# Issuing V chunks under a queue limit, and a longer lag for the Q/K loads, in a scheduled attention and expert kernel

## The chip, the cores and the metric

The kernel runs on one core of one Trainium2 chip. The metric is the device time of one execution in microseconds (us), the median of several. TensorE is called PE, VectorE DVE, ScalarE ACT, GpSimd POOL and SyncE SP in the profile.

## The reference, cut to what matters

Eight batches, eight heads, 576 positions, head width 64. Attention has a decay from `f`; each batch is then sent through one of eight two-layer experts, chosen by its mean.

```python
q, k, v: (8, 8, 576, 64)   f: (8, 8, 576)   x: (8, 576, 512)   w1: (8, 512, 1024)   w2: (8, 1024, 512)
scores = q @ k.T / 8 ;  cum = cumsum(log(clip(f)))
scores = where(causal, -1e9, scores + cum[i] - cum[j])
attn = softmax(scores) ;  x = attn @ v             # heads side by side: 512 columns
e_idx = argmax(x.mean(positions) @ w_gate)         # one expert for each batch
out = gate * (relu(x @ w1[e_idx]) @ w2[e_idx])
```

## The kernel before

Heads are worked in 16 groups of four (a "quad"; two quads to a batch, four "exps" to a quad). A quad goes through these steps: DVE transposes K and Q; PE makes scores into one shared buffer (`ps_s`, "s=1" below); ACT takes the exp and so frees that buffer; POOL masks it; POOL weighs V by the decay; PE multiplies the masked exps with V ("PV"). Each batch then has a first expert layer (`H`, line L535) and a second (`O`, L550). While one batch's layers run, the next batch's quads run in between.

The order of all of this is decided when the kernel is built. Every operation is an `Op` with an engine, an estimated duration, what it comes after, and a priority. A class `Order` runs a model of the engines and of the DMA queues, and emits instructions in the order in which they start in that model. `behind` means "not before that other operation has been issued".

```python
FILL = 60.0
PM0 = 10.0
LAG = 2
# ... in Order:
    def can(self, op, now):            # are the buffers that op takes free?
        need = {}
        for ring, key in op.takes:
            need[ring] = need.get(ring, 0) + 1
            if ring in self.turn and self.turn[ring][0] != key:
                return False
        return all(sum(t <= now for t, _ in self.free[r]) >= n for r, n in need.items())
# ... a DMA's landing is modelled by self.queues[e]: one list for SP, ACT and POOL each
    RINGS = dict(raw=4, qt=2, vf=2, vb=3, e=2, lr=3, x=4, w=3, h=2, o=6, s=1, bank=4, gate=4)
```

V of a batch is loaded in five chunks of positions: c0, c2 and c4 are issued by SyncE, c1 and c3 by ScalarE. The first four are 256 KB each, in pieces of 256 bytes. Results are stored by SyncE. K, Q and the weights are loaded by GpSimd.

```python
    def load_v(op, b, c):
        eng = nc.scalar if op.engine == "ACT" else nc.sync
        t = VF[od.slot(("vf", b))]
        if c < 4:
            eng.dma_start(t[:, c, :, :], v[b, :, P * c:P * c + P, :].rearrange("h p e -> p h e"))   # L274
        else:
            eng.dma_start(t[64:P, 4, :, :], v[b, :, 512:576, :].rearrange("h p e -> p h e"))        # L276
# ...
            loads_v[b, c] = od.add(f"v{b}{c}", "ACT" if c % 2 else "SP", .4 if c % 2 else .5, lambda op, b=b, c=c: load_v(op, b, c),
                                   prio=6 * b + c * .1 - 8, takes=(("vf", b),) if c == 0 else (), lands=1.4 if c < 4 else .7, grain=.022, ...)
# ... scores (L370), exp (L376), PV (L412), first layer (L535), second layer (L550) are Ops too
            for g in range(5, NQ):     # when quad g's K and Q may be loaded
                raws[g, 1].behind = [ld2] if g < 6 else [wvs[g - LAG][0]]
```

The softmax here doesn't subtract the row's maximum and nothing guards it: scores larger than these inputs give would overflow.

## Time and profile before

| | before |
|---|---|
| time, median (lowest to highest) of 3 | 266.82 us (265.76 to 266.83) |
| span of the profiled run | 263.9 us |
| PE busy | 235.2 us, 89% |
| PE idle after 41 us, all gaps | 15.2 us |
| ACT waiting for a DMA, before an exp | 4.7 + 4.5 us |

The page of the profile gives the busy time of each engine, then busy tenths in 40 slices of 6.6 us. PEclk is the clock that TensorE was granted, in tenths.

```profile
span 263.9 us, 7930 instructions
PE 235.2 (89%) x3325; PEld 152.6 (58%) x3325; DVE 110.9 (42%) x297; ACT 174.9 (66%) x261; POOL 128.2 (49%) x195
...
PE   7778998939999999499899976799999999999991
...
PEclk9975999988999999799999997999999999999998
```

PE is the busiest engine. It has three holes in mid-kernel: the digits 3, 4 and the 7 6 7 at about 53, 106 and 154 to 166 us. After each, the granted clock dips too.

The list of waits says who made whom wait (total us, times, longest us).

```profile
POOL e L383 <- ACT e L376: 76.9, 34, 8.0
...
PE ps_s L370 <- ACT e L376: 15.1, 12, 4.1
...
DVE kt L361 <- DMA rawk<-in_k_dram: 4.7, 3, 1.8
ACT e L376 <- DMA vf<-in_v_dram: 4.7, 1, 4.7
ACT e L376 <- DMA out_dram<-otile: 4.5, 1, 4.5
```

The largest total, 76.9 us of GpSimd, costs nothing by itself: GpSimd is half idle. The two lines at the bottom are one wait each. An exp reads `ps_s` and no V or output, so it can't depend on these DMAs. What waited was the instruction ahead of it in ScalarE's stream, as ScalarE's timeline shows (start, duration, what; in brackets the idle time before it; ACTq is an issue by ScalarE).

```profile
50.56 0.42 ACT L422 ACTIVATE lr<-lr 128x256 f32<-128x256 f32 x1
55.27 0.37 ACTq L274 DMA_DIRECT2D vf<-in_v_dram  x1
55.70 1.66 ACT L376 ACTIVATE e<-ps_s 128x1792 bf16<-128x1792 f32 x1 [4.71 <-DMA vf<-in_v_dram]
...
101.39 1.66 ACT L376 ACTIVATE e<-ps_s 128x1792 bf16<-128x1792 f32 x1 [0.61 <-PE ps_s L370]
107.16 0.37 ACTq L274 DMA_DIRECT2D vf<-in_v_dram  x1
107.58 1.45 ACT L376 ACTIVATE e<-ps_s 128x1536 bf16<-128x1536 f32 x1 [4.53 <-DMA out_dram<-otile]
```

Both times ScalarE stood before the issue of a V chunk. TensorE's timeline in the first block and in the third hole:

```profile
57.41 0.94 PE L370 MATMUL ps_s<-qt,kt 32*128 32x448 bf16 x8 [4.06 <-ACT e L376]
58.28 2.88 PE L535 MATMUL ps_w<-xT,w1e 128*128 128x288 bf16 x12
...
157.94 0.58 PE L370 MATMUL ps_s<-qt,kt 32*128 32x448 bf16 x8 [1.83 <-ACT e L376]
160.34 0.83 PE L370 MATMUL ps_s<-qt,kt 32*128 32x320 bf16 x16 [1.82 <-ACT e L376]
```

In the first block TensorE lost 4.06 us, then ran twelve matmuls in 2.88 us. In the third hole nothing was blocked. Only scores and exps were left in the order, and these take turns on the one buffer.

The chain that ended last names the two transfers behind the blocks (start, us, what):

```profile
34.76 20.42 DMA vf<-in_v_dram
55.27 0.37 ACTq L274
...
92.62 14.48 DMA out_dram<-otile
107.16 0.37 ACTq L274
```

A V load issued by SyncE at 34.76 held up an issue of ScalarE at 55.27, and a store issued by SyncE at 92.62 held up the one at 107.16.

### The profile page before, as it was taken

What the parts mean: (1) busy time and instruction counts of PE and PEld (TensorE: products, weight loads), DVE (VectorE), ACT (ScalarE), POOL (GpSimd) and SP (SyncE); (2) the same over time, 40 slices, a digit from 0 to 9 for tenths busy, and PEclk for the clock granted to TensorE, in tenths of its full rate; (3) what the DMA queues carried; (4) which work ended last, traced back from release to release, by engine and by line L of the source; (5) the groups of instructions that cost most, each with busy time, mean ns of one, the idle gap of its engine ahead of it and who ended that gap; (6) DMA issues with size and microseconds to landing.
All of it is one profiled execution on the core that took longest, in us unless ns stands there. A gap on an engine that the chain in (4) does not pass through costs nothing.

```text
span 263.9 us, 7930 instructions
## 1 busy us (share of the span) xinstructions
PE 235.2 (89%) x3325; PEld 152.6 (58%) x3325; DVE 110.9 (42%) x297; ACT 174.9 (66%) x261; POOL 128.2 (49%) x195
## 2 busy tenths in 40 slices
PE   7778998939999999499899976799999999999991
PEld 2326636716478646377478622768467756876940
DVE  3974553444045855155148600774057623410000
ACT  2398677658486774586586856678487867754930
POOL 4187099304976492207950638608933772140000
PEclk9975999988999999799999997999999999999998
DMA  6988979991999999954999998695997299049832
GB/s 114 225 136 174 189 112 211 212 225 19 180 264 221 225 217 251 232 131 71 219 251 227 201 224 142 111 255 84 201 259 167 37 211 255 6 66 224 211 102 87
DMA packets 57370, 45.84 MB, mean 174 GB/s; under 512 B 39600, under 2 KB 41648, under 8 KB 57328
## 3 DMA queue, kind: packets, MB, share of 16 engines
q0 software_dynamic: 13584, 26.22, 55.6%
q1 hardware_dynamic: 27104, 14.85, 22.5%
q10 hardware_dynamic: 16640, 4.20, 8.1%
q8 instruction: 28, 0.46, 0.7%
q14 instruction: 14, 0.11, 0.2%
HBM read 62.03 MB, written 9.44 MB: 271 GB/s over the span
## 4 chain that ended last, share of the span: by engine, by line
PE 53%; DMA 21%; ACT 8%; DVE 6%; issue 6%; POOL 4%; POOLq 0%; ACTq 0%; SPq 0%; DVEq 0%
PE ps_w L535 18%; PE ps_w L550 14%; PE ps_w L412 9%; DMA vf<-in_v_dram 8%; DMA rawk<-in_k_dram 7%; PE ps_s L370 7%; DMA out_dram<-otile 5%; ACT e L376 5%; PE ps_w L553 2%; PE ps_w L492 2%; ACT e L379 2%; DVE kt L361 2%; DVE qt L361 1%; POOL vb L396 1%; PE ps_w L612 1%
## 5 line engine op out<-in xcount | busy, mean ns | idle before, releaser
L376 ACT ACTIVATE e<-ps_s 128x1792 bf16<-128x1792 f32 (+2 forms) x61 | 91.9, 1507 | 31.1 <-PE ps_s L370 18.0
L383 POOL TENSOR_SCALAR_AFFINE_SELECT e<-e 128x512 bf16<-128x512 bf16 x64 | 41.4, 650 | 80.6 <-ACT e L376 76.9
L535 PE MATMUL ps_w<-xT,w1e 128*128 128x288 bf16 x512 | 74.4, 295 | 1.6 <-DMA w1e<-in_moe_w_dram 1.1
L535 PEld LDWEIGHTS <-w1e 128*128 128x128 bf16 x512 | 61.5, 143 | 11.0 <-issue 5.0
L550 PE MATMUL ps_w<-w2e,h1T 128*128 128x512 bf16 x256 | 60.1, 384 | 0.0
L428 DVE SCALAR_TENSOR_TENSOR xT<-ps_w,lr 128x256 bf16<-128x256 f32 (+1 forms) x64 | 26.9, 454 | 56.7 <-ACT lr L422 55.9
L370 PE MATMUL ps_s<-qt,kt 32*128 32x448 bf16 (+3 forms) x728 | 34.2, 291 | 15.6 <-ACT e L376 15.1
L543 ACT ACTIVATE h1T<-ps_w,gate_b 128x288 bf16<-128x288 f32 x72 | 35.4, 500 | 13.2 <-PE ps_w L535 12.6
L541 DVE TENSOR_SCALAR h1T<-ps_w,gate_b 128x288 bf16<-128x288 f32 x56 | 28.0, 511 | 32.7 <-PE ps_w L535 32.7
L550 PEld LDWEIGHTS <-h1T 128*128 128x128 bf16 x256 | 23.3, 98 | 29.6 <-issue 4.2
L370 PEld LDWEIGHTS <-kt 32*128 32x128 bf16 x768 | 16.5, 96 | 35.5 <-issue 32.9
L412 PE MATMUL ps_w<-e,vb 128*32 128x320 bf16 (+4 forms) x1024 | 29.6, 257 | 2.4 <-DVE xT L428 1.2
L562 ACT COPY otile<-ps_w 128x512 f32<-128x512 f32 (+1 forms) x29 | 15.8, 546 | 23.8 <-PE ps_w L550 22.6
L396 POOL TENSOR_TENSOR vb<-vf,WF 128x512 bf16<-128x512 f32 x29 | 30.5, 1053 | 0.4
L412 PEld LDWEIGHTS <-vb 128*32 128x32 bf16 x1024 | 22.3, 100 | 5.5 <-issue 3.5
L361 DVE STREAM_TRANSPOSE kt<-rawk 128x576 f32<-128x576 f32 x16 | 20.0, 1250 | 7.6 <-DMA rawk<-in_k_dram 4.7
L515 POOL DMA_DIRECT2D w1e<-in_moe_w_dram x14 | 10.4, 743 | 20.4 <-DVE gate_b L506 15.3
L361 DVE STREAM_TRANSPOSE qt<-rawq 128x576 f32<-128x576 f32 x16 | 19.9, 1246 | 0.0
L412 PE MATMUL ps_w<-e,WB 128*32 128x192 bf16 (+4 forms) x512 | 17.8, 261 | 0.4 <-ACT lr L417 0.2
L417 ACT ACTIVATE lr<-ps_w 128x256 f32<-128x256 f32 (+1 forms) x32 | 13.2, 414 | 6.4 <-PE ps_w L412 6.3
L612 PE MATMUL ps_w<-still 128*128 128x512 bf16 x55 | 15.8, 433 | 1.4 <-DVE still L289 1.4
L412 PEld LDWEIGHTS <-WB 128*32 128x32 bf16 x512 | 10.6, 99 | 9.0 <-issue 7.1
(55 smaller groups left out, 144.3 us busy)
## 6 DMA issues: line engine op xcount, KB each, us to landing
out_dram<-otile SPq DMA_DIRECT2D x32, 256.0 KB, 7.4
w1e<-in_moe_w_dram POOLq DMA_DIRECT2D x14, 512.0 KB, 7.5
w2e<-in_moe_w_dram POOLq DMA_DIRECT2D x14, 512.0 KB, 13.5
rawk<-in_k_dram POOLq DMA_DIRECT2D x16, 288.0 KB, 10.7
rawq<-in_q_dram POOLq DMA_DIRECT2D x16, 288.0 KB, 11.8
vf<-in_v_dram ACTq DMA_DIRECT2D x16, 256.0 KB, 9.3
vf<-in_v_dram SPq DMA_DIRECT2D x16, 256.0 KB, 10.2
vf<-in_v_dram SPq DMA_DIRECT2D x8, 128.0 KB, 9.3
```

The source lines that it names most:

```text
L361: nc.vector.transpose(dst, raw)
L370: nc.tensor.matmul(ps[h][:, col:col + i1 - i0], kt[32 * h:32 * h + 32, KLO[c]:KLO[c] + P, r], qt[32 * h:32 * h + 32, i0:i1, r], start=(r = ...
L376: nc.scalar.activation(e, PS_S[:, :, 0:WIDTH[s]], AF.Exp, scale=0.125)
L383: nc.gpsimd.affine_select(out=e[:, :, 0:128], in_=e[:, :, 0:128], pattern=[[0, 4], [1, 128]], channel_multiplier=-1, base=0, compare_op=AL ...
L396: eng.tensor_tensor(vb[:, c, :, :], vf[:, c, h, :], WF[:, b, c, h].unsqueeze(3).to_broadcast([P, 2, 4, D]), op=ALU.mult)
L412: nc.tensor.matmul(ps[32 * h:32 * h + 32, lo - i0:hi - i0], lhs, e[s][:, h, col:col + hi - lo], start=(n == 0), stop=(n == len(parts) - 1) ...
L428: nc.vector.scalar_tensor_tensor(XT[od.slot(("x", b))][:, mm, i0:i1], ps[:, 0:i1 - i0], LN_SCALE, LR[od.slot(("lr", (g, blk)))][:, 0:i1 - ...
L535: nc.tensor.matmul(ps[:, 0:288], lhs, xT[:, m, 288 * half:288 * half + 288], start=(m == 0), stop=(m == 3))
L541: nc.vector.tensor_scalar(dst, ps[:, 0:288], g[:, 0:1], 0.0, op0=ALU.mult, op1=ALU.max)
L543: nc.scalar.activation(dst, ps[:, 0:288], AF.Relu, scale=g[:, 0:1])
L550: nc.tensor.matmul(ps, h[:, j, P * sb:P * sb + P], r, start=(j == 0), stop=(j == 7))
L612: od.filler = lambda i: nc.tensor.matmul(PS_W[i], still[:, 0:P], still[:, 0:512])
```

## The change

The intent as stated: a V chunk goes to a hardware queue only while that queue holds at most two others, so that the issue does not block ScalarE; and the Q/K loads are held back by three quads, not two. (In the code, K and Q of quad g now wait for the weighing of V of quad g - 3 in place of g - 2, so they may be issued one quad earlier.) `runs` is a size that counts against RUNS for each queue of the scheduler's model: 64 for a V chunk (32 for c4), 8 for a store. By these sizes the limit of 130 is tighter than the stated intent: a full chunk is issued while its queue holds at most one other full chunk and no store (64 + 64 = 128). The limit acts on the model's queues when the order is built. No work is added or removed; only the order can change.

```diff
+RUNS = 130
-LAG = 2
+LAG = 3
 ...
     def can(self, op, now):
         need = {}
+        if op.runs and sum(q[3].runs for q in self.queues[op.engines[0]]) + op.runs > RUNS:
+            return False
 ...
-             ... lands=1.4 if c < 4 else .7, grain=.022,                                  # V chunk
+             ... lands=1.4 if c < 4 else .7, grain=.022, runs=64 if c < 4 else 32,
 ...
-             ... lands=.7, grain=.086)                                                    # store
+             ... lands=.7, grain=.086, runs=8)
```

The changed file is three lines longer, so L370, L376, L412, L535 and L550 become L373, L379, L415, L538 and L553.

More of the change, by code (lines that the diff above doesn't have):

```diff
@@ L37, with __init__ @@
 FILL = 60.0
+RUNS = 130
 PM0 = 10.0
-LAG = 2
+LAG = 3
 class Op:
-    def __init__(self, name, engines, us, fn, after=(), prio=0.0, takes=(), gives=(), lands=None, grain=None, behind=()):
+    def __init__(self, name, engines, us, fn, after=(), prio=0.0, takes=(), gives=(), lands=None, grain=None, runs=0, behind=()):
         self.name, self.us, self.fn, self.prio = name, us, fn, prio
@@ L49, in __init__ @@
         self.after, self.takes, self.gives, self.lands = list(after), takes, gives, lands
-        self.end, self.grain = None, grain
+        self.end, self.grain, self.runs = None, grain, runs
         self.other, self.fellow, self.behind, self.issued = (), (), behind, None
@@ L310, in fast_path @@
             loads_v[b, c] = od.add(f"v{b}{c}", "ACT" if c % 2 else "SP", .4 if c % 2 else .5, lambda op, b=b, c=c: load_v(op, b, c), prio=6 * b + c * .1 - 8,
-                                   takes=(("vf", b),) if c == 0 else (), lands=1.4 if c < 4 else .7, grain=.022,
+                                   takes=(("vf", b),) if c == 0 else (), lands=1.4 if c < 4 else .7, grain=.022, runs=64 if c < 4 else 32,
                                    after=[marks[b]] if c == 0 and b in marks else [], behind=[loads_v[b, c - 1]] if c else [])
@@ L610, in fast_path @@
                         takes=(("o", (b, sb)),), gives=(("bank", ("o", b, sb)),))
-            od.add(f"D{b}{sb}", "SP", .5, lambda op, b=b, sb=sb: store(op, b, sb), prio=pm + 3.4 + .5 * n, after=[oc], gives=(("o", (b, sb)),), lands=.7, grain=.086)
+            od.add(f"D{b}{sb}", "SP", .5, lambda op, b=b, sb=sb: store(op, b, sb), prio=pm + 3.4 + .5 * n, after=[oc], gives=(("o", (b, sb)),), lands=.7, grain=.086, runs=8)
     od.filler = lambda i: nc.tensor.matmul(PS_W[i], still[:, 0:P], still[:, 0:512])
```

## The prediction

> **What bounds it now.** From about 131 us on, the chain of waits is almost all TensorE (busy 44.5 of 45 us in the stretch 190:235), so there only TensorE's idle time can be won. By timeline and busy-by-stretch table it stands still three times:
> - 53.3 to 57.4 us: idle 4.06 us; ScalarE did nothing from 51.0 to 55.3.
> - 105.7 to 109.1 us: idle 3.34 us; ScalarE nothing from 103.0 to 107.2.
> - 154 to 166 us: 7.5 of 12 us busy; only score and exp steps were left in the order, alternating on the one score buffer, because the next V product was ordered late.
>
> The waits list gives both ScalarE gaps to a DMA: 4.7 and 4.5 us of idle before an exp. In both, ScalarE's next instruction is a V load. After each pause the granted clock is 0.5 for 3.4 us (12 first-layer matmuls took 2.88 us instead of 1.55). The Trainium skill, "TensorE: Matmul & The Clock Gate", Part 1, says this: half rate after an idle window of about 3.4 us; the trace agrees. So the blocks cost 4.1 + 1.7 and 3.3 + 1.7 us: together nearly 11 us.
>
> **A doubt about the reason.** The blocked issues don't look like a full queue: each carries a semaphore that an earlier transfer still held. The issue at 55.27 uses that of the V load issued at 34.75, which landed at 55.18; the one at 107.16 that of a store issued at 92.61, landed 107.10 (its semaphore wait is 5.7 us long). Eight semaphores rotate over both hardware queues, so an issue waits for the transfer eight before it. SyncE does show issues of 3 to 10 us, perhaps a full queue, but it only delays V and stores.
>
> **What the change moves.** No work is added or removed. In the built order V of batch 3 is issued not all at the 16th exp but at the 20th to 25th, mixed with stores; later V loads also come later and spread out. Their semaphore predecessors are then mostly long landed: neither block should recur. Exposed: ScalarE's loads of batches 4 and 5 near exps 33 to 35, whose predecessors are stores issued only 2 to 3 exps before (0 to 4 us). K/Q loads move one quad earlier (quad 6 at exp 15, not 20, ahead of the second expert's weights), ending delays like the 15.3 us from issue to landing at 68.9 us; TensorE was busy then, so that is worth under 2 us.
>
> Given back: V is used 4 to 5 exps after issue instead of 7 to 16, and hardware V loads take 6 to 25 us under load. The order still has a run of exps with little else (34 to 39, in place of 41 to 48), so I expect the 154 to 166 stall to move, not vanish.
>
> **Sum.** 266.8 - 11 (both blocks) - 1 (K/Q) + 4 (late V, a residual block) = about 259 us; 80% range 251 to 266. Chances: faster by over 2% 0.62, within 2% 0.31, slower 0.07.
>
> **What would show it.** Right: no ScalarE idle over 3 us before an exp with a DMA as releaser before 110 us; two fewer half-clock windows; TensorE busy within 4 us of 235; a score/exp-only stretch near exp 35. Wrong: ScalarE still waiting for a semaphore at a V load, or GpSimd waiting several us for V at its weighing, holding up masks behind it.
>
> **What would make it wrong.** V landing late at batches 3, 4, 5 turns the blocks into V waits (about 265); or the new order fills the 154 to 166 hole too (about 250).

## The result, and the profile after

Ratios are the mean time of one kernel's fast runs over that of the other's fast runs of the same rounds, so they are not quite the ratio of the medians quoted beside them.

| | before | after |
|---|---|---|
| time, median (lowest to highest) of 4 | 266.29 us (264.84 to 266.83) | 255.85 us (255.62 to 257.98) |
| ratio to before | | 0.963 (0.957 to 0.970) |
| span of the profiled run, mean clock | 263.9 us, 0.958 | 253.9 us, 0.964 |
| PE busy | 235.2 us | 230.4 us |
| PE idle after 41 us | 15.2 us | 9.3 us |
| half-clock windows between 50 and 240 us | 3 of 3.4 us | 1 of 6.8 us |

The page of the kernel after:

```profile
span 253.9 us, 7942 instructions
PE 230.4 (91%) x3309; PEld 152.7 (60%) x3324; DVE 108.3 (43%) x293; ACT 176.8 (70%) x265; POOL 128.1 (50%) x195
...
PE   7778988999999999998399899999899999999990
...
PEclk9985899999999999999679999999999999999999
```

The holes at 53 and 106 us are gone, and so is the one at 154 to 166. There is a new one at 120 to 127 us (the digits 8 3, clock 6 7).

Its list of waits:

```profile
POOL e L386 <- ACT e L379: 72.8, 31, 5.9
...
ACT e L379 <- PE ps_s L373: 12.2, 23, 1.0
PE ps_s L373 <- ACT e L379: 9.9, 11, 1.8
DVE kt L364 <- DMA rawk<-in_k_dram: 8.5, 3, 4.7
```

No line of ScalarE waiting for a DMA before an exp is left. On ScalarE's timeline an exp now follows the issue of a V chunk without idle time:

```profile
79.98 0.38 ACTq L277 DMA_DIRECT2D vf<-in_v_dram  x1
80.56 1.66 ACT L379 ACTIVATE e<-ps_s 128x1792 bf16<-128x1792 f32 x1
```

TensorE's longest wait for an exp fell from 4.1 to 1.8 us. DVE's wait for K grew from 4.7 to 8.5 us.

TensorE's timeline in the new hole:

```profile
121.28 0.58 PE L373 MATMUL ps_s<-qt,kt 32*128 32x448 bf16 x8 [1.33 <-ACT e L379]
123.62 0.94 PE L373 MATMUL ps_s<-qt,kt 32*128 32x448 bf16 x8 [1.76 <-ACT e L379]
126.32 0.83 PE L373 MATMUL ps_s<-qt,kt 32*128 32x320 bf16 x16 [1.76 <-ACT e L379]
```

It has the same form as the old hole at 154: scores and exps take turns, until PV products are ready at 127.08. The granted clock is halved from 123.1 on, for 6.8 us. Idle time is 4.85 us.

A third comparison, used for every run below: when does TensorE start the second layer of each batch, read from the first matmuls of that layer in the trace (us)?

| batch | 0 | 1 | 2 | 3 | 4 | 5 | 6 | 7 |
|---|---|---|---|---|---|---|---|---|
| before | 64.2 | 90.5 | 122.4 | 148.2 | 183.1 | 209.3 | 233.9 | 250.0 |
| after | 59.0 | 85.4 | 103.7 | 145.5 | 172.4 | 199.2 | 223.4 | 239.6 |

The gain is 5.2 us at batch 0 and 10.7 at batch 4; from there on nothing more is won or lost. (Batches 2 and 3 stand differently in the two orders, so their columns don't compare.)

The chain after begins differently, as it should when the blocks are gone:

```profile
34.30 6.63 DMA w1e<-in_moe_w_dram
40.97 0.93 PE ps_w L538 x6
41.90 0.51 PE ps_s L373 x7
```

After the first expert's weights it runs through TensorE; the V load and the store are not in it.

### The profile page after: what moved, and what is told of

It reads as the page before. It is cut to its first block, busy times and chain, and to the rows that moved or that the text cites. A ratio compares the mean times of both kernels' runs of the same rounds, so it can differ in the third digit from the quotient of the medians.

```text
span 253.9 us, 7942 instructions
## 1 busy us (share of the span) xinstructions
PE 230.4 (91%) x3309; PEld 152.7 (60%) x3324; DVE 108.3 (43%) x293; ACT 176.8 (70%) x265; POOL 128.1 (50%) x195
## 4 chain that ended last, share of the span: by engine, by line
PE 64%; DMA 14%; ACT 9%; issue 5%; DVE 3%; POOL 2%; POOLq 1%; ACTq 0%
PE ps_w L538 22%; PE ps_w L553 16%; PE ps_w L415 12%; PE ps_s L373 9%; DMA rawk<-in_k_dram 8%; DMA w1e<-in_moe_w_dram 6%; ACT e L379 6%; PE ps_w L556 2%; PE ps_w L495 2%; ACT e L382 2%; DVE h1T L544 1%; PE ps_w L615 1%; ACT otile L565 1%; DVE qt L364 1%; POOLq L514 1%
## 5 line engine op out<-in xcount | busy, mean ns | idle before, releaser
L379 ACT ACTIVATE e<-ps_s 128x1792 bf16<-128x1792 f32 (+2 forms) x61 | 91.9, 1506 | 14.7 <-PE ps_s L373 12.2
L538 PE MATMUL ps_w<-xT,w1e 128*128 128x288 bf16 x512 | 72.6, 290 | 1.4 <-DMA w1e<-in_moe_w_dram 1.0
L538 PEld LDWEIGHTS <-w1e 128*128 128x128 bf16 x512 | 60.5, 142 | 9.5 <-issue 4.7
L553 PE MATMUL ps_w<-w2e,h1T 128*128 128x512 bf16 x244 | 56.2, 379 | 1.5 <-issue 1.3
L373 PE MATMUL ps_s<-qt,kt 32*128 32x448 bf16 (+3 forms) x728 | 34.1, 290 | 10.3 <-ACT e L379 9.9
L544 DVE TENSOR_SCALAR h1T<-ps_w,gate_b 128x288 bf16<-128x288 f32 x58 | 29.3, 513 | 32.9 <-PE ps_w L538 32.2
L565 ACT COPY otile<-ps_w 128x512 f32<-128x512 f32 (+1 forms) x35 | 19.2, 549 | 32.9 <-PE ps_w L553 31.1
L546 ACT ACTIVATE h1T<-ps_w,gate_b 128x288 bf16<-128x288 f32 x70 | 34.5, 500 | 10.5 <-PE ps_w L538 9.8
L553 PEld LDWEIGHTS <-h1T 128*128 128x128 bf16 x256 | 23.7, 98 | 30.1 <-issue 3.5
L373 PEld LDWEIGHTS <-kt 32*128 32x128 bf16 x768 | 16.3, 95 | 28.2 <-issue 25.7
L415 PE MATMUL ps_w<-e,vb 128*32 128x320 bf16 (+4 forms) x1024 | 30.1, 261 | 0.1
L415 PEld LDWEIGHTS <-vb 128*32 128x32 bf16 x1024 | 22.3, 102 | 4.0 <-issue 1.6
L415 PE MATMUL ps_w<-e,WB 128*32 128x192 bf16 (+4 forms) x512 | 18.4, 268 | 0.2
L615 PE MATMUL ps_w<-still 128*128 128x512 bf16 x51 | 15.1, 446 | 2.1 <-DVE still L292 1.4
L415 PEld LDWEIGHTS <-WB 128*32 128x32 bf16 x512 | 10.9, 101 | 8.8 <-issue 6.6
```

The lines of the kernel that those rows point to most:

```text
L373: nc.tensor.matmul(ps[h][:, col:col + i1 - i0], kt[32 * h:32 * h + 32, KLO[c]:KLO[c] + P, r], qt[32 * h:32 * h + 32, i0:i1, r], start=(r = ...
L379: nc.scalar.activation(e, PS_S[:, :, 0:WIDTH[s]], AF.Exp, scale=0.125)
L415: nc.tensor.matmul(ps[32 * h:32 * h + 32, lo - i0:hi - i0], lhs, e[s][:, h, col:col + hi - lo], start=(n == 0), stop=(n == len(parts) - 1) ...
L538: nc.tensor.matmul(ps[:, 0:288], lhs, xT[:, m, 288 * half:288 * half + 288], start=(m == 0), stop=(m == 3))
L544: nc.vector.tensor_scalar(dst, ps[:, 0:288], g[:, 0:1], 0.0, op0=ALU.mult, op1=ALU.max)
L546: nc.scalar.activation(dst, ps[:, 0:288], AF.Relu, scale=g[:, 0:1])
```

## The experiments

Two questions were open. What held ScalarE: a full queue, as the change's intent says, or the completion semaphores? And where do the 10 us come from: the two blocks alone, or the new order too?

**What the trace says on the first.** Each hardware DMA (one issued by SyncE or ScalarE) carries a completion semaphore. In these programs eight of them are used in turn by both engines together. So an issue needs the semaphore of the hardware DMA eight before it in the program. "Slack" here is the time from the landing of that earlier DMA to the issue. No issue of ScalarE in the kernel before has a smaller slack than the three smallest shown; all the others have 5 us or more:

| kernel | issue by ScalarE | DMA eight before | landed | slack |
|---|---|---|---|---|
| before | 49.45 | V load of SyncE, 34.33 | 42.87 | 6.57 |
| before | **55.27** | V load of SyncE, 34.76 | 55.18 | **0.10** |
| before | 81.00 | store, 67.80 | 74.96 | 6.04 |
| before | **107.16** | store, 92.62 | 107.10 | **0.07** |
| before | 135.25 | store, 125.93 | 134.26 | 0.99 |
| after | all after 50 us | | | 2.43 or more |

The wait instruction before the second blocked issue is recorded as well: it names that semaphore (and one more, whose last DMA had landed by 99.39) and lasts 5.73 us, from 101.40. A queue reading does not explain this, since ScalarE's own issues never take over 0.69 us once they start in these two kernels. On SyncE some V issues do take 3 to 10.7 us by themselves, in most cases while two or more V chunks issued there before are still moving (at 75.71 and 105.57 in the kernel before, 3.60 and 3.85 us, it was one, with stores; 70.63 took 10.68 us in the kernel after, in spite of the limit). That does look like a full queue, but it is SyncE's.

All runs below gave correct results. Single kernels scatter by about 1 to 2% from run to run, so differences under 1% are not read.

### The limit alone (LAG stays 2)

```diff
-LAG = 3
+LAG = 2
```

> The changed kernel with K/Q held back by 2 quads again: only the limit on V chunks is left. Its order issues V of batch 3 at the 19th to 20th exp instead of the 16th, so the V loads that held its semaphores have landed. If the blocks at ScalarE are the cost (my theory): no ScalarE idle over 3 us before an exp with a DMA as releaser, and most of the 10.4 us gain: 256 to 261 us; its order has a longer run of exps with no V product (32 to 40), so 1 to 4 us may be given back against the changed kernel. If the K/Q part does the work (rival): 264 us or more.

Measured: 259.77 us (255.88 to 261.60; two of four runs slow), ratio 0.985 (0.973 to 0.996). In the profiled run, at 255.88 us, no issue blocked ScalarE, and the score and exp hole stood at 147 to 154 us with 1.34 + 1.76 + 1.76 us of idle. Second layers started at 171.0 (batch 4) and 240.4 (batch 7), within 1.5 us of the kernel after. So the limit alone takes both blocks away. The timed runs were too scattered to say whether it gives all of the gain.

### The lag alone (no limit)

```diff
-LAG = 2
+LAG = 3
```

> The kernel before with K/Q held back by 3 quads and no limit on V chunks. If the V limit is what pays: ScalarE still waits several us for a semaphore at one or two V loads and the time is 261 to 267 us. If the K/Q part pays by itself, or if any reshuffling of the order moves the blocked loads away: 255 to 260 us. The trace decides between the last two: a ScalarE wait for a DMA gone in spite of bursts of V would mean that the limit is not needed for it.

Measured: 265.35 us (263.76 to 267.56), ratio 1.004 (0.990 to 1.018). The time fell into the first range of the expectation, but for another reason than the one given there: in its trace ScalarE is no longer blocked. Moving the K/Q loads had moved the V issues as well; the ones at 56.06 and 108.40 us had slack of 11 and 13 us, and the one at 58.59 barely escaped, with 0.10. What was won was lost elsewhere. TensorE's timeline of this kernel, in the middle and near the end:

```profile
128.41 0.52 PE L370 MATMUL ps_s<-qt,kt 32*128 32x320 bf16 x16 [1.76 <-ACT e L376]
130.49 0.47 PE L370 MATMUL ps_s<-qt,kt 32*128 32x192 bf16 x16 [1.56 <-ACT e L376]
132.83 2.56 PE L535 MATMUL ps_w<-xT,w1e 128*128 128x288 bf16 x10 [1.87 <-ACT otile L562]
...
240.01 2.38 PE L535 MATMUL ps_w<-xT,w1e 128*128 128x288 bf16 x9 [2.61 <-DMA w1e<-in_moe_w_dram]
```

Its second layers started 4.7 us ahead of before at batch 6 (229.2 against 233.9), but only 0.5 ahead at batch 7 (249.5 against 250.0): the last batch waited 2.61 us for its first-layer weights and then ran 3.4 us at half clock. Between, it had a hole of its own (1.76 + 1.56 + 1.87 us). Over the whole trace TensorE stood idle for 14.9 us after 41 us, against 15.2 before, and between 50 and 245 us the clock was at half for 13.7 us, against 10.2. So "the blocks are gone" is not enough for a gain; the rest of the order has to hold.

### The blocks alone: before's order, every V chunk issued by SyncE

```diff
-        eng = nc.scalar if op.engine == "ACT" else nc.sync
+        eng = nc.sync
```

> The kernel before, every engine's order as it was, but all V loads are issued by SyncE in the same place of its order; ScalarE issues none. If ScalarE standing at its V loads is the cost: TensorE's two pauses at 53 to 57 and 106 to 109 us vanish and the time falls by 7 to 11 us, to 256 to 260 us, with the hole near 154 us still there; V may land later, as one queue carries it all. If the new order of work is what pays and not the blocks: within 3 us of before.

Measured: 258.34 us (257.68 to 260.11), ratio 0.978 (0.966 to 0.990). This is the cleanest measure of the blocks, for the order on every other engine is that of before. Second layers start, against before: 4.7 us earlier at batch 0, 9.4 at batch 2, 9.4 at batch 3, 7.7 at batch 4 and 7.6 at batch 7. So the first block cost 4.7 us and the second another 4.7, and 1.7 us was given back in the old hole, which is still there:

```profile
148.58 0.57 PE L370 MATMUL ps_s<-qt,kt 32*128 32x448 bf16 x8 [1.83 <-ACT e L376]
150.98 0.83 PE L370 MATMUL ps_s<-qt,kt 32*128 32x320 bf16 x16 [1.82 <-ACT e L376]
```

The same two gaps as before's at 157.94 and 160.34, now with half-clock windows of 6.8 and 3.4 us in place of one of 3.4. (The last section says what can make the difference.)

### A block put back by bytes that fill no queue

Into the kernel after: six loads of 32 bytes on SyncE, behind V of batch 3. They move the rotation, but hardly load a queue.

```diff
+    pads = [const.tile([1, 8], fp32, name=f"pad{i}") for i in range(6)]
 ...
+        if b == 3 and c == 4:
+            for t in pads:
+                nc.sync.dma_start(t, f[0, 0:1, 0:8])
```

> The changed kernel with six extra loads of 32 bytes on SyncE behind V of batch 3; they add next to nothing to the queues but turn the eight semaphores on by six, so that ScalarE's second V load of batch 3 (issued at 80.0 us) must wait for a V load on SyncE that landed at 87.4 us. If the rotation of semaphores blocks (my theory): ScalarE stands 5 to 8 us there, TensorE pauses, and the time rises by 2 to 7 us, to 258 to 263 us. If a full queue is what blocks (rival): no wait of ScalarE there and within 1 us of the changed kernel.

Measured: 262.61 us (261.75 to 264.00), ratio 0.995 (0.983 to 1.006) to before, where the kernel after has 0.963 to 0.972. ScalarE's and TensorE's timelines of this kernel (its lines are numbered seven higher than before's; the V load is four higher):

```profile
79.82 0.99 ACT L550 ACTIVATE h1T<-ps_w,gate_b 128x288 bf16<-128x288 f32 x2 [0.40 <-PE ps_w L542]
86.34 0.37 ACTq L278 DMA_DIRECT2D vf<-in_v_dram  x1
86.82 1.66 ACT L383 ACTIVATE e<-ps_s 128x1792 bf16<-128x1792 f32 x1 [6.00 <-DMA vf<-in_v_dram]
```
```profile
88.53 0.83 PE L377 MATMUL ps_s<-qt,kt 32*128 32x320 bf16 x16 [5.30 <-ACT e L383]
```

A block of 6.00 us was made, and TensorE lost 5.30. The six small issues make a staircase that follows the landings of the DMAs eight before, to within 0.03 us once SyncE is past its long V issue:

| issue | at | DMA eight before | landed |
|---|---|---|---|
| SyncE, small load 3 | 83.18 | store, 63.26 | 83.17 |
| SyncE, small load 4 | 84.02 | store, 65.65 | 84.00 |
| SyncE, small load 5 | 84.66 | store, 66.92 | 84.64 |
| SyncE, small load 6 | 85.29 | store, 68.66 | 85.28 |
| ScalarE, V chunk | 86.34 | V load of SyncE, 69.68 | 86.32 |

ScalarE's own queue was empty all this time: its last V issue, at 59.28, had landed by 62.18. This settles it for this block: the semaphore's turn held the issue, not the queue that it goes to.

### Before's first block, moved by the count of small loads

Into the kernel before: five or six 32-byte loads on SyncE, ahead of V of batch 3. With five, the blocked issue should again meet a V load; with six, one of the small loads.

```diff
+    pads = [const.tile([1, 8], fp32, name=f"pad{i}") for i in range(5)]    # or 6
 ...
+        if b == 3 and c == 0:
+            for t in pads:
+                nc.sync.dma_start(t, f[0, 0:1, 0:8])
```

> The kernel before with five extra loads of 32 bytes on SyncE ahead of V of batch 3. The rotation then gives ScalarE's first V load of batch 3 the semaphore of its own V load c3 of batch 2, which landed at 56.5 us, and its second one that of an extra load. If the rotation blocks (my theory): the first block stays and is 1 to 3 us longer, from about 49 to 56.5 us; time 264 to 270 us. If a full queue blocks (rival): the block is as before, 51.0 to 55.3 us, and so is the time.

> The same with six extra loads instead of five: one load of 32 bytes more. Now both of ScalarE's V loads of batch 3 follow extra loads in the rotation. If the rotation blocks (my theory): the first block is gone, TensorE does not pause at 53 to 57 us, and the time falls by 3 to 6 us against before, to 259 to 263 us, the second block (near 100 us) staying. SyncE's own V loads of batch 3 then wait to about 56 us, which should not matter. If a full queue blocks (rival): same as before and as with five.

Measured with five: 266.90 us (264.97 to 270.62), ratio 1.010 (0.995 to 1.024). ScalarE's recorded wait names the predicted semaphores, the last to come being that of its own V load, which landed at 56.74, and takes 6.68 us from 50.08; TensorE's gap is 5.38 us in place of 4.06. As expected; but as that load is ScalarE's own, this run alone would not exclude a full queue of ScalarE. With six, the issue went out at 55.47 while that load was still moving (it landed at 56.74).

Measured with six: 263.79 us (262.92 to 269.68), ratio 0.998 (0.985 to 1.011). The block did not go, against the expectation. ScalarE's timeline with six (lines numbered four higher than before's):

```profile
49.67 0.50 ACT L547 ACTIVATE h1T<-ps_w,gate_b 128x288 bf16<-128x288 f32 x1 [0.29 <-PE ps_w L539]
55.47 0.38 ACTq L278 DMA_DIRECT2D vf<-in_v_dram  x1
55.89 0.38 ACT L421 ACTIVATE lr<-ps_w 128x256 f32<-128x256 f32 x1 [5.72 <-DMA pad<-in_f_dram]
```

The profile names the small load as what held ScalarE. It was issued at 40.30; the issue instruction ended at 41.91; part of its semaphore's count came at 42.12, but the 32 bytes moved at 54.41 and the count was complete at 55.39, and ScalarE's wait for that semaphore ended at 55.41. Four small loads issued by SyncE between 38.94 and 43.01 all moved their bytes at 54.41 to 54.44, so they had stood behind something in SyncE's queue: most likely the V chunks issued just before them, which landed at 43 to 57 us. So a 32-byte transfer can hold an issue for 5 us. The Trainium skill says as much of both halves: "DMA: Bandwidth & Descriptors", section "Queues, rings and completion order", that each DMA engine takes descriptors in ring order; section "Why a DMA increments its semaphore by 16 and not by 1", that the issuer writes at once the counts for the DMA engines that a small transfer doesn't use. The trace agrees, with 42.12 and 55.39 us. The miss was in the expectation's guess of when it lands, not in the rotation.

### The changed kernel again, and with every V chunk on SyncE

```diff
 # after_again: no edit.   after_v_sync:
-        eng = nc.scalar if op.engine == "ACT" else nc.sync
+        eng = nc.sync
```

> The changed kernel itself, on the same chip as the next three, as their yardstick: 255 to 258 us, 3 to 4% under before, with TensorE's one hole near 120 us and no ScalarE wait for a DMA.

> The changed kernel with all V loads issued by SyncE in the same order. As ScalarE no longer waits at V loads in the changed kernel, nothing is left to win: within 2 us of it, unless V on one queue lands later and is missed (then 1 to 4 us slower). A gain of over 2 us would mean that ScalarE's V issues still cost something that I overlooked.

Measured: 257.50 us (256.51 to 261.44, the highest slow), ratio 0.972 (0.960 to 0.985), and 256.43 us (254.25 to 257.87), ratio 0.972 (0.961 to 0.982). No difference: in the new order ScalarE has nothing left to be freed of. This is also what the Trainium skill leads one to expect ("DMA: Bandwidth & Descriptors", section "Issuing engines are not separate DMA queues"): which engine issues changes only sequencer time, and transfers share the same 16 DMA engines. In the order of the kernel before, the same edit was worth 2.2%, because there ScalarE stood waiting for semaphores.

### A looser limit, to fill the hole

In the built order of the kernel after, six to seven exps go by between the PV products of one quad and those of the next, in the worst places; with RUNS=194 and LAG=2 it is at most five after the first batch. So that order should have no hole. It was tried with V on SyncE, with a limit of 170 as well, and with V issued as in the kernel after.

```diff
-RUNS = 130
-LAG = 3
+RUNS = 194        # r170_l2_sync: 170
+LAG = 2
 ...               # r194_l2_sync and r170_l2_sync also:
-        eng = nc.scalar if op.engine == "ACT" else nc.sync
+        eng = nc.sync
```

> Two separate causes, taken on together: V issued by SyncE (no block at ScalarE can come from it), and the limit loosened from 130 to 194 with K/Q held back by 2 quads, an order whose runs of exps without a V product are at most 4 long after the first batch (the changed kernel has one of 7 and one of 6, before one of 7 or more). If the hole near 120 us (4.9 us idle and 6.8 us at half clock) is made by such a run of exps: no hole after 60 us longer than 1 us in sum, and 248 to 253 us. If holes come from somewhere else (late V): 254 to 260 us.

> The same with the limit at 170, another order with runs of at most 5. If the length of the run is what counts: 248 to 254 us, as the one with 194; if the orders differ by chance in what they meet: 250 to 260 us.

> The order of the first of these three, with ScalarE issuing its share of V. In its rotation ScalarE's V loads of batch 5 follow stores issued shortly before them. If the rotation catches it: a ScalarE idle of 2 to 5 us at one of its V loads and 2 to 5 us more than with SyncE; if not: within 1.5 us of it.

Measured: 255.74 us (253.99 to 256.93), ratio 0.961 (0.954 to 0.967); 255.22 us (254.06 to 258.19), ratio 0.959 (0.953 to 0.965); 254.00 us (252.80 to 256.41), ratio 0.954 (0.948 to 0.960). The granted clock of the third, over the slices of the page:

```profile
PEclk9985899999999999999999999999999999999998
```

The hole is gone (from 41 us on, the clock is full up to the last slice), but little came of it. The profiled run of the third starts batch 7's second layer at 240.4, against 239.6 for the kernel after: it is behind by 4.5 us at batch 1 (89.9 against 85.4), where the V chunks go out sooner and smaller gaps stand (1.53 us at 81.4, 1.11 at 88.4), and then wins that back. Two cautions: this trace is of the slowest of the third's six runs (256.41 us; the others took 252.80 to 255.26), and the trace of the first, at 253.99 us, starts batch 7's second layer at 238.4. So filling the hole seems to have cost part of its worth elsewhere; how much is not shown. The first two missed their expected ranges (248 to 253 and 248 to 254 us). The third was not caught by the rotation, as the second branch of its expectation has it. The profiled run with the limit of 170 was slow and is not read.

### The changed kernel, five rounds

> The changed kernel once more, in five rounds, so that its ratio to before has an interval as narrow as those of the three orders of the last call (0.954 to 0.961): 0.963 to 0.972. Below 0.958, those orders are no faster than the change; above 0.965, the one with ScalarE issuing (0.954) is faster by about 1%.

Measured: 256.19 us (255.29 to 258.25), ratio 0.972 (0.965 to 0.978). The hole is at 120.3 to 126.7 us, with the same three gaps as before (1.34 + 1.76 + 1.76). Against this the version with RUNS=194 and LAG=2 has a lower ratio (0.954), and the intervals don't overlap; but the two were timed in different calls, whose runs of the kernel before differ by almost 2 us (267.47 and 265.61), and its one trace, of its slowest run, shows no earlier finish. The medians differ by 2.2 us. It is probably the fastest version here, by 1 to 2%, but this was not tested within the same rounds.

## Why the prediction was right

**That the blocks come from the semaphores' turn, and not from a full queue: right.** Shown by the staircase, where six 32-byte loads put a block back, and by the one block that a 32-byte load held. The stated intent of the change names the wrong cause for ScalarE; the change works because issuing V later and spread among stores leaves each issue of ScalarE with a landed predecessor (slack of 2.43 us or more in the profile, 1.80 in that of after_again). That is a by-product: the limit does not see semaphores, and the lag alone escaped a block by 0.10 us.

**That neither block recurs: right.** ScalarE's two waits of 4.7 and 4.5 us are gone from the list.

**"The blocks cost ... together nearly 11 us": right in kind, a little high.** Measured alone, with before's order, they cost 9.4 us up to batch 3. The estimate was idle time plus half of each 3.4 us window at half clock. Of the half clock the Trainium skill says that it follows one idle window of about 3.4 us ("TensorE: Matmul & The Clock Gate", Part 1), and the trace agrees for the first block, where the 3.4 us just before the half clock were all idle. For the second less was enough: TensorE was busy for 16% of them. How the 1.4 us between 10.8 and 9.4 arise was not measured.

**"K/Q (1)": not seen.** The K load's median time to landing went from 10.7 to 11.0 us, DVE's wait for K grew from 4.7 to 8.5 us, and the chain after still holds a K load of 15.21 us, at 150.94. TensorE's gaps at that time are under 1 us, so this cost little.

**"+ 4 (late V, a residual block)": this is the term of the sum that was mis-sized; it came out near zero.** No residual block came: the predicted candidates near exps 33 to 35 had slack of 8 us and more. GpSimd did not stand for late V, for with only one or two V chunks under way at a time, those issued between 92.8 and 118.0 us landed in 3 to 8 us. By the table of second layers, the kernel after is 3.0 us ahead of the one with the blocks alone taken out (10.7 against 7.7 at batch 4). So 9.4 us were won by the blocks, and about 1.3 us net in these two traces at the hole: the gaps are as large (4.85 + 0.97 us, against 5.6 us in before's order without the blocks), but the old hole drew 10.2 us of half clock there, and the new one 6.8. That these 1.3 us belong to the new order is not shown. With the same gaps the old hole drew only 3.4 us in the kernel before, and the new one 3.4 us in after_again; and the timed ratios overlap (0.978, 0.966 to 0.990, for the blocks alone; 0.972, 0.965 to 0.978, for the kernel after in five rounds). So the removal of the blocks is what is shown to pay.

**"I expect the 154 to 166 stall to move, not vanish ... near exp 35": right.** It moved to 120 to 127 us. The busy times by stretch show the old one and the new (us from and to, length, then busy us and count of each engine, and the granted clock). Of the kernel before, and of the kernel after:

```profile
154.00:166.00 12.00, 7.46 (x80) 2.98 (x79) 0.29 (x1) 7.31 (x8) 7.70 (x12) 0.86 0.87 165
```
```profile
119.00:127.00 8.00, 3.14 (x51) 1.36 (x49) 2.99 (x4) 5.10 (x6) 7.66 (x11) 0.76 1.08 212
154.00:166.00 12.00, 12.00 (x279) 9.08 (x279) 5.24 (x18) 10.35 (x17) 7.15 (x11) 1.00 1.12 250
```

TensorE (the first busy figure) was idle 4.5 of 12 us in the old hole, and 4.9 of 8 in the new one; the old place is full.

**"TensorE busy within 4 us of 235": right, though the profile says 230.4.** That trace lacks 12 of 256 matmuls of L553. The two other profiled runs of the same kernel, after_again and after_five, have all 3,324 matmuls and show 231.5 and 232.0 us, within 4. Most of what is left comes from the clock: between 50 and 240 us TensorE was busy at half clock for 9.3 us before, and for 2.9 and 3.8 us in those two, which by half of the difference (an estimate) is about 3 us.

**"two fewer half-clock windows": right by count, 3 and then 1, but the one is twice as long.** In time it is 10.2 and then 6.8 us (3.4 in after_again).

What stays open: how much of the gain the lag adds to the limit. Alone it gave nothing, and the limit alone scattered by 2%.

## What to carry to other kernels

When an engine stands at a DMA issue, look up which semaphore the wait names and which earlier transfer holds it: it may belong to another queue, and a 32-byte load can hold it as well as a large one. Then issue from an engine off the critical path, or put the issue where the transfer that many places before has long landed. And after a wait is removed, look where TensorE idles next: of the orders without the blocks, one gained nothing, because, by its trace, a hole elsewhere and a late weight load took it back.

## What the Trainium skill lacked or had wrong

- "DMA: Bandwidth & Descriptors", section "Issuing engines are not separate DMA queues", says that the sequencer's time to initiate a DMA is usually small relative to the DMA itself. The issue instruction on ScalarE took 0.37 us here, but the wait for a completion semaphore still held by an earlier DMA (in four of the five blocks looked at here, one of SyncE) took 4.5 to 6.7 us of a compute engine. Neither this page nor any other that was consulted tells of completion semaphores being taken in turn by both issuing engines (eight of them in this program), nor that an issue then waits for the DMA eight before.
- The same page gives no depth at which an issue itself becomes slow. On SyncE, V issues of 128 or 256 KB in 256-byte pieces took 3 to 10.7 us (70.63 us in the kernel after: 10.68), mostly when two or more V chunks issued there were still moving. The cause of these was not tested.
- "TensorE: Matmul & The Clock Gate", in its closing table, advises no idle gaps over about 3 us, and its Part 1 speaks of one idle window. Here the clock was halved for 6.8 us from 123.1 us on with no gap over 1.76 us: TensorE was busy for 3.14 of 8 us in that stretch. The page's section on PSUM-queue cycling does say that frequent short idle times make the clock oscillate, but gives no share. The 13 traces of fast runs give one, counted from 42 us to 16 us before the end: the clock changes on a fixed grid of 3.41 us. Of the windows at full clock, all 17 in which TensorE was busy for at most 45% were followed by half clock, and none of the 692 in which it was busy for 60% or more; of the five between, three were. So the same gaps cost more or less by how they fall on the grid: with gaps of 1.34 + 1.76 + 1.76 us the same kernel had 6.8 us at half clock in after_five and 3.4 in after_again.
